# Chunk 4 of images 1 to 6: loads of u and z placed behind a transposed tile, a transpose of u moved from step 10 to step 24

## The chip, the cores and the metric

The kernel runs on one core of one Trainium2 chip. The metric is the device time of one execution in microseconds (us); lower is better. Five engines work side by side, each through its own queue in order: PE (TensorE, matrix products; its weight loads are listed as PEld), DVE (VectorE), ACT (ScalarE), POOL (GpSimd) and SP (SyncE, which only issues transfers). Transfers (DMAs) are issued from the queues of SP, POOL and ACT and land later; whoever needs the data waits for the landing.

## The reference

A gated attention unit without softmax, followed by a two-layer network with a quick GELU, over 8 images of 3008 tokens:

```python
# u, v: (8, 3008, 256), z: (8, 3008, 64), w_in: (256, 2048), w_out: (2048, 256)
scores = (1.0 / S) * np.matmul(z, z.transpose(0, 2, 1))
attn = np.maximum(scores, 0.0) ** 2
out = np.matmul(attn, v)
x = (u * out).reshape(B * S, D)

h = x @ w_in
g = h * (1.0 / (1.0 + np.exp(-1.702 * h)))
return (g @ w_out).astype(np.float32)
```

The scores are symmetric, since queries and keys are both z. The result has float32 elements, 24064 x 256.

## The kernel before, in words

The images (b = 0 to 7) go one after the other. The 3008 query rows of an image are six chunks of 512 rows (i = 0 to 5, NCH = 6), the last one padded; the keys are NJ = 24 blocks of 128. For each pair of blocks a *unit* (i, jp) of scores is made: PE multiplies (L246), ACT takes the ReLU into a tile rl (L267; L257 for a folded half), DVE squares it into a tile a (L272, L281, L284; L258 for the half). Because the scores are symmetric, half of the blocks are not computed a second time but turned by transposing DMAs on SP's queue: `turn_unit` (L309) writes the tiles tt, L274 the tile ad, L288 the tile al. For chunk 4 the turned units are jp = 10 and jp = 11; they fill the first and the second half of the tile TT[b, 4, 5].

The order of the work is written out by hand. `attend` gives the steps of a chunk (matmuls of the attention with v, L528); the loop over n walks through them, and tables keyed by (chunk i, step n) say what else is put in ahead of a step: SCHED how many units are taken (those of chunk 4 at (3, 3), (3, 10), (3, 17) and, with one of chunk 5, (3, 24), in the order of `pieces`), LOAD when a chunk's u is loaded (`load_u`, L206, four DMAs on POOL's queue), TURN when DVE turns it 32 by 32 (`turn_u`, L213, tile uq into ut). The list LAST2 holds the two last stores of the image before: a DVE transpose (yo, L858) and four or more DMAs on SP (L868) each.

In images 1 to 6 chunk 4 is done in another way (`split`, `attend_split`): a Strassen-like scheme of seven products P1 to P7 on sums of blocks. Its matmuls are L439. The sums of the scores, S1 to S4 (tile sa, L391 to L395; S3 in place, L382), are made on DVE at the places that `fills` lists; for the last third of the keys they are S1 at (4, 12), S2 at (4, 14), S4 at (4, 16) and (4, 18), S3 at (4, 20) and (4, 22), and they read TT[b, 4, 5]. The products end in L451 (ACT) and L457 (DVE) on tiles ya, which share their buffers with rl, and in the gates L459, L461, L453, which multiply with the turned u. In the same chunk 16 groups of the network's first layer run between the steps (`up_group`: PE L583, ACT gelu L596 into gf, DVE L602 into gt, then sums L718 to L722).

`load_z` prepares the next image. For each half of the blocks it loads z (`stage_z`, POOL's queue, L160 and L163), copies it beside itself on POOL (L173), and transposes it into ZT by a DMA on SP's queue (L174). ZT of the next image is read first by the scores that are taken in chunk 5 at step 2. `load_u` of chunk 5 stands at (4, 29); its turn is at (5, 8).

The places that matter here, for images 1 to 6:

- POOL's queue: u of chunk 4 at (3, 44); at (4, 2) z half 0, copy 0, z half 1, copy 1; u of chunk 5 at (4, 29). Each copy waits for its half's landing. Before it, POOL has a marker (L88) that waits for PE in the middle of chunk 3.
- SP's queue around the start of chunk 4: four stores, ad, two halves of tt, two of al, the next stores, the two transposes of ZT.
- DVE's queue: yo of the first store, then the squares of chunk 4's units; the turn of u at (4, 10), ahead of S1.

Of the kernel before, what the change touches and what calls it, by code (L numbers as in the profile page):

```python
# [10 lines left out]
F16 = mybir.dt.float16  # L11
P = 128
# [3 lines left out]
def kernel(  # L16
# [20 lines left out]
    NJ = (S + P - 1) // P  # L37
# [3 lines left out]
    NCH = (S + CH - 1) // CH  # L41
    CB = CH // P
    NU = NJ // 2
# [12 lines left out]
    dve, act, pe, sp, pool = nc.vector, nc.scalar, nc.tensor, nc.sync, nc.gpsimd  # L56
# [9 lines left out]
    pw = ctx.enter_context(tc.tile_pool(name="pw", bufs=2))  # L66
# [14 lines left out]
    ZT, V16, UQ, UT, XT, unit, TT = {}, {}, {}, {}, {}, {}, {}  # L81
# [74 lines left out]
    def stage_z(b, n0, **home):  # L156
        zst = ZS[n0] = pw.tile([P, NU, 2, DQK], F16, name="zst", **home)
        full = min(NU, NJ - 1 - n0)
        src = z[b, n0 * P:(n0 + full) * P].rearrange("(n p) d -> p n d", p=P)
        pool.dma_start(zst[:, :full, 0, :], src)  # L160
        if full < NU:
            for h in range(2):
                pool.dma_start(zst[h * SREM:(h + 1) * SREM, full, 0, :], z[b, S0:S])  # L163

    def load_z(b):
        ZT[b] = pz.tile([P, NJ, P], F16, name="ZT", tag="ZT")
        if b == 1:
            stage_z(b, NU, tag="y")
        for n0 in range(0, NJ, NU):
            if b > 1:  # L170
                stage_z(b, n0, tag="y")
            zst = ZS[n0]
            pool.tensor_copy(zst[:, :, 1, :], zst[:, :, 0, :])  # L173
            sp.dma_start_transpose(ZT[b][:, n0:n0 + NU], zst.rearrange("p n c d -> p (n c d)"))  # L174
# [24 lines left out]
    def load_u(b, i):  # L199
        eng = pool if b else sp  # L200
        n = width(i)
        uq = pu.tile([P, CH // QW, QW, NCC], F32, name="uq", tag="uq")
        src = u[b, i * CH:i * CH + n].rearrange("(q t) c -> t q c", t=QW)
        for k in range(P // QW):
            cs = slice(k * NCC * QW, (k + 1) * NCC * QW)
            eng.dma_start(uq[k * QW:(k + 1) * QW, :n // QW].rearrange("t q c k -> t q (c k)"), src[:, :, cs])  # L206
        UQ[b, i] = uq
# [22 lines left out]
    def turned(b, i):  # L230

        return i < NCH - 1 and (b > 0 or i > 3)
# [102 lines left out]
    def split(b, i):  # L335

        return i == NCH - 2 and 0 < b < B - 1
# [127 lines left out]
    def fills(b):  # L465

        VT.clear()
        SA.clear()
        at = {(0, 19): [lambda: pool.tensor_copy(VZ[TOP], V16[b][TOP, NJ - 1])]}
        slots = [(0, n) for n in (20, 23, 26, 28)] + [(1, n) for n in (27, 31, 35, 39, 43)]  # L470
        slots += [(2, n) for n in (19, 21, 23)]
        ops = [op for t in range(3) for op in value_forms(b, t)]
        slots += [(2, n) for n in (28, 33, 38, 43)] + [(3, n) for n in (30, 34, 41, 44)]
        slots += [(4, n) for n in (12, 12, 14, 14, 16, 18, 20, 22)]
        ops += [op for t in range(3) for op in score_forms(b, t)]
        assert len(ops) == len(slots)
        for where, op in zip(slots, ops):
            at.setdefault(where, []).append(op)
        return at

    def full(b):

        return NCH - 2 if b < B - 1 else NCH - 1
# [349 lines left out]
    LAST2 = []  # L833
# [42 lines left out]
    def pieces(b, i):  # L876

        lst = [(i, jp) for jp in range(2 * i, NU)]
        if i == NCH - 1:
            return [(i, jp) for jp in range(2 * i) if not turned(b, jp // 2)] + lst  # L880
        if b == 0:
            return lst[-2:] + lst[:-2] if turned(b, i) else lst
        if split(b, i):
            return [lst[0], lst[2], lst[3], lst[1]]
        k = max(len(lst) - 6, 2)
        return lst[:k] + lst[-2:] + lst[k:-2]

# [12 lines left out]
    TURN0 = {(i, (38, 28)[i] if i < 2 else NJ + 4 if i < NCH - 1 else 12): i for i in range(NCH)}  # L900
    LOAD0 = {(1, 14): 2, (1, 40): 3, (4, 4): 4, (4, 36): 5}
    TURN = {(1, NJ + 4): 2, (2, NJ + 4): 3, (4, 10): 4, (5, 8): 5}
    LOADW = {
        (2, 16): 0, (3, 0): 2, (3, 9): 1, (3, 41): 3, (4, 28): 4, (4, 34): 5, (4, 40): 6, (5, 0): 7,
    }
    CASTW = {(3, 8): 0, (3, 40): 2, (4, 8): 1, (4, 14): 3}
    LOAD = {(3, NJ + 20): 4, (4, NJ + 5): 5}

    FIRST_ZT, FIRST_CAST = {12: 4, 20: 5}, {5: 4, 13: 5}
    SCHED0 = {  # L910
# [14 lines left out]
    def fill(b):  # L925
        assert not queue
        queue.extend(u_ for i in range(NCH) for u_ in pieces(b, i))
# [28 lines left out]
    for b in range(B):  # L956
        nup = NCH * NFG
        more = b + 1 < B
        sched = SCHED0 if b == 0 else SCHED if more else SCHED_LAST
        turn, load = (TURN, LOAD) if b else (TURN0, LOAD0)  # L960
        head = 0
        for i in range(NCH):
            host = b + 1 if more and i == NCH - 1 else b
            if host > b:
                fill(host)
                LATE.append(host)
            if i == 0 and split(b, NCH - 2):
                extra = fills(b)
            for n, step in enumerate(attend_split(b, i) if split(b, i) else attend(b, i, b == 0 and i == 0)):
                if b == 0 and i == 0 and n in (5, 24):  # L970
                    load_u(0, n // 24)
                if b == 0 and i == 0 and n == 2:
                    copies = first_zt(3)
                if b == 0 and i == 0 and n == 3:
                    copies()
                if b == 0 and i == 0 and n in FIRST_CAST:
                    first_cast(FIRST_CAST[n], True)
                if b == 0 and i == 0 and n in FIRST_ZT:
                    first_zt(FIRST_ZT[n])()
                if (i, n) in turn:  # L980
                    turn_u(b, turn[i, n])
                if (i, n) in ((3, 3), (3, 26) if more else (4, 14)) and LAST2:
                    LAST2.pop(0)()
                if (i, n) == (0, 22) and COPY:
                    COPY.pop(0)()
                if (i, n) in load:
                    load_u(b, load[i, n])
                if b == 0 and (i, n) in CASTW:
                    cast_w(CASTW[i, n])
                if b == 0 and (i, n) in LOADW:  # L990
                    load_w(LOADW[i, n])
                if b == 0 and (i, n) == (NCH - 2, 6):
                    stage_z(1, 0, tag="yo", bufs=1)
                if more and (i, n) == (NCH - 2, 2 if b else 16):
                    load_z(b + 1)
                if b == 0 and i == NCH - 1 and n in (8, 30, 42):
                    wsums.pop(0)()
                take(host, sched[i].get(n, 0))
                if split(b, NCH - 2):
                    for op in extra.get((i, n), ()):  # L1000
                        op()
                if split(b, i):
                    step()
                if i == full(b) and n >= HEAD and (n - HEAD) * LAGY // (2 * NJ - 10) >= head and head < LAGY:
                    up_group(b, head)
                    head += 1
                if not split(b, i):
                    step()
        late.sort(key=lambda t: t[0])
        if more:  # L1010
            for i in range(2):
                load_u(b + 1, i)
            for n0 in range(0, NJ, VB):
                load_v(b + 1, n0)
        prods = products(b)
        for q in range(head, nup):
            if more and q in (head + 14, head + 20):
                k = int(q == head + 20)
                turn_u(b + 1, k)
                load_u(b + 1, k + 2)  # L1020
            up_group(b, q)
            if b == 0 and q == head + 3:
                wsums.pop(0)()
            prods.pop(0)()
            for a_ in AFTER:
                a_[0] -= 1
            while AFTER and AFTER[0][0] < 0:
                AFTER.pop(0)[1]()
            if q >= 44 and late:
                late.pop(0)[1]()  # L1030
        steps = prods
        for step in steps:
            step()
            for sum_ in [SUMS.pop(0) for _ in range(min(len(SUMS), 1 + (len(SUMS) > 4)))]:
                sum_[2]()
            for _, turn_it in [late.pop(0) for _ in range(min(len(late), 1 + (len(steps) < 10)))]:
                turn_it()
        LATE.clear()
        if more:
            while late:  # L1040
                late.pop(0)[1]()
            take(b + 1, 2)
# [30 lines left out]
```

## Time and profile before

Three runs took 1172.9, 1173.56 and 1173.79 us; the median is 1173.56.

| what | value |
|---|---|
| the profiled execution | 1173.48 us |
| its span, from the first instruction to the last | 1171.4 us |
| granted TensorE clock | 1.000 |
| first L439 matmul of chunk 4, images 1 to 6 | 205.16, 350.43, 493.34, 638.32, 780.48, 927.60 us |
| landing of a tt transpose after its issue, all 232 | 3.1 / 3.4 / 11.5 us (min / median / max) |
| u load, one of four: POOL's time to issue it | 649 ns (median) |
| turn of u on DVE, 48 of them | 1236 ns (median) |
| POOL's copy of a z half, 14 of them | 958 ns (median) |

Lines of the profile name a line of the kernel, an engine, an operation, the tile written and the tiles read, the count, and times. In the list of waits the columns are: who waited, for whom, us in total, how often, the longest one. In a table of windows each row is a stretch of time, followed by each engine's busy time and instructions, the granted clock, the share of the DMA engines and their rate. In a timeline each row is a start, a duration, an engine, a line, an operation and, in brackets, the engine's idle time before it and what ended it. An engine's idle time costs nothing unless PE comes to wait for it: PE is busy 99% of the span.

### The profile page before, as it was taken

The page shows a single profiled execution, that of the slowest core. Times are in us where ns is not written, and L with a number is a line of the kernel's source. Part 1 is how long each engine was busy: PE and PEld are TensorE (multiplying, and loading weights), DVE is VectorE, ACT ScalarE, POOL GpSimd, SP SyncE. Part 2 cuts the span into 40 slices and gives each one's busy share as a digit, 9 for nine tenths or more (in the row PEclk, how much of TensorE's full clock was granted, in tenths as well). Part 3 has the DMA queues.
Part 4 walks back from the last instruction along what each step waited for, and adds up shares of the span by engine and source line. Part 5 has one row for each costly group of instructions (what it writes and reads, how often), then busy time and mean ns, then how long its engine had stood idle before and what let it go on. Part 6 is the DMA issues. An engine that isn't in the chain of part 4 may idle for free.

```text
span 1171.4 us, 21514 instructions
## 1 busy us (share of the span) xinstructions
PE 1163.4 (99%) x8212; PEld 590.0 (50%) x8212; DVE 961.4 (82%) x1596; ACT 841.9 (72%) x959; POOL 215.2 (18%) x301
## 2 busy tenths in 40 slices
PE   9999999999999999999999999999999999999998
PEld 3544455644455445554445545555444554544446
DVE  7789878988789886899868997779977899664776
ACT  7888864788647886478864787657876588672785
POOL 3033201232012320142101421014210241001000
PEclk9999999999999999999999999999999999999999
DMA  9996399854998559976499655995559955697023
GB/s 222 201 168 96 79 172 158 100 94 92 169 156 101 90 108 170 153 104 87 97 172 153 107 86 111 170 139 103 90 101 170 153 106 85 119 165 142 1 36 73
DMA packets 459032, 143.53 MB, mean 123 GB/s; under 512 B 424624, under 2 KB 453040, under 8 KB 458928
## 3 DMA queue, kind: packets, MB, share of 16 engines
q1 hardware_dynamic: 402464, 102.36, 53.6%
q0 software_dynamic: 55104, 38.49, 21.8%
q8 instruction: 64, 1.05, 0.4%
q10 hardware_dynamic: 1360, 1.31, 0.4%
q14 instruction: 40, 0.33, 0.1%
HBM read 60.29 MB, written 24.64 MB: 73 GB/s over the span
## 4 chain that ended last, share of the span: by engine, by line
PE 92%; DVE 3%; DMA 3%; ACT 1%; issue 1%; SPq 0%; DVEq 0%; ACTq 0%
PE o L528 32%; PE hg L583 26%; PE st L756 23%; PE sc L246 6%; PE oz L439 4%; DMA tt<-a 2%; PE st L804 1%; PE yp L730 1%; DVE gt L602 1%; DMA out_dram<-yo 1%; ACT rl L267 1%; ACT gf L596 0%; DVE vt L362 0%; SPq L868 0%; PE w L101 0%
## 5 line engine op out<-in xcount | busy, mean ns | idle before, releaser
L596 ACT ACTIVATE gf<-hg 128x1024 f32<-128x1024 f32 (+1 forms) x384 | 383.4, 1002 | 119.7 <-PE hg L583 100.0
L267 ACT ACTIVATE rl<-sc 128x1024 f16<-128x1024 f32 (+1 forms) x301 | 288.8, 992 | 153.7 <-PE sc L246 109.9
L583 PE MATMUL hg<-xt,W 128*128 128x512 f16 (+1 forms) x1408 | 353.5, 374 | 0.2
L528 PEld LDWEIGHTS <-V 64*128 64x128 f16 (+1 forms) x3810 | 206.6, 94 | 201.1 <-POOLq L88 6.1
L528 PE MATMUL o<-a,V 64*128 64x512 f16 (+3 forms) x2254 | 290.5, 368 | 0.4 <-DVE a L281 0.4
L602 DVE TENSOR_SCALAR gt<-gf 128x1024 f16<-128x1024 f32 (+1 forms) x288 | 204.8, 712 | 66.4 <-ACT gf L596 63.7
L206 POOL DMA_DIRECT2D uq<-in_u_dram x168 | 117.2, 706 | 725.4 <-DVE a L284 394.1
L281 DVE TENSOR_TENSOR a<-rl 128x1024 f16<-128x1024 f16 (+1 forms) x266 | 176.2, 673 | 77.2 <-ACT rl L267 76.1
L583 PEld LDWEIGHTS <-W 128*128 128x128 f16 x1536 | 149.4, 98 | 156.5 <-issue 3.3
L528 PE MATMUL o<-tt,V 64*128 64x512 f16 (+1 forms) x1278 | 166.9, 376 | 0.0
L246 PE MATMUL sc<-ZT 64*128 64x512 f16 (+3 forms) x688 | 117.3, 356 | 0.7 <-ACT ZT L145 0.3
L756 PEld LDWEIGHTS <-WT 128*128 128x128 f16 x736 | 71.9, 98 | 79.6 <-issue 0.6
L600 ACT ACTIVATE gt<-gf 128x1024 f16<-128x1024 f32 (+1 forms) x96 | 98.1, 1022 | 3.1
L756 PE MATMUL st<-gt,W 128*128 128x512 f16 (+1 forms) x368 | 89.9, 370 | 0.0
L756 PE MATMUL st<-s,WT 128*128 128x512 f16 (+1 forms) x368 | 89.1, 370 | 0.0
L756 PE MATMUL st<-gt,WT 128*128 128x512 f16 (+1 forms) x368 | 88.8, 370 | 0.0
L756 PEld LDWEIGHTS <-W 128*128 128x128 f16 x552 | 53.8, 98 | 58.3
L858 DVE STREAM_TRANSPOSE yo<-y 128x1024 f32<-128x1024 f32 (+1 forms) x46 | 56.0, 1218 | 8.5 <-DMA out_dram<-yo 5.8
L718 DVE TENSOR_TENSOR s<-gt 128x1024 f16<-128x1024 f16 (+1 forms) x92 | 61.3, 666 | 1.1
L720 DVE TENSOR_TENSOR s<-s,gt 128x1024 f16<-128x1024 f16 (+1 forms) x92 | 61.0, 663 | 1.2
L773 DVE SCALAR_TENSOR_TENSOR y<-st,y 128x512 f32<-128x512 f32 (+1 forms) x69 | 45.7, 662 | 19.6 <-PE st L756 18.8
L722 DVE TENSOR_TENSOR s<-gt,s 128x1024 f16<-128x1024 f16 (+1 forms) x92 | 59.4, 657 | 2.2 <-DVE s L720 1.4
(100 smaller groups left out, 916.8 us busy)
## 6 DMA issues: line engine op xcount, KB each, us to landing
out_dram<-yo SPq DMA_DIRECT2D x156, 128.0 KB, 2.8
uq<-in_u_dram POOLq DMA_DIRECT2D x140, 128.0 KB, 3.5
V<-in_v_dram POOLq DMA_DIRECT2D x35, 256.0 KB, 6.0
tt<-a SPq DMA_TRANSPOSE x232, 3.4
uq<-in_u_dram POOLq DMA_DIRECT2D x28, 112.0 KB, 4.6
out_dram<-yo SPq DMA_DIRECT2D x28, 96.0 KB, 3.5
uq<-in_u_dram SPq DMA_DIRECT2D x20, 128.0 KB, 4.3
wst<-in_moe_w_in_dram POOLq DMA_DIRECT2D x4, 512.0 KB, 5.1
```

The costliest lines, as they stand in the source:

```text
L206: eng.dma_start(uq[k * QW:(k + 1) * QW, :n // QW].rearrange("t q c k -> t q (c k)"), src[:, :, cs])
L246: pe.matmul(sc[:, r, :q1 - q0], zt[h, 2 * kp + r, :], zt[h].rearrange("d n p -> d (n p)")[:, q0:q1], start=True, stop=True,)
L267: act.activation(rl[:, :, :n], sc[:, :, :n], AF.Relu, scale=csc)
L281: dve.tensor_tensor(a[:, :, :n], rl[:, :, :n], rl[:, :, :n], ALU.mult)
L528: ins = pe.matmul(acc[c][:, :n], channels(V16[b][h, j], c), weights(b, i, j)[h], start=(k, m) == first[c], stop=(k, m) == final[c],)
L583: pe.matmul(hg[:, e, :n], W1[:, c, ff * P:(ff + 1) * P], XT[b, i][:, c, :n], start=(c == 0), stop=(c == NCC - 1),)
L596: act.activation(gf[:, :, :n], hg[:, :, :n], AF.Gelu_apprx_sigmoid, scale=1.0 / FSC)
L600: act.activation(g, gf[:, :, :n], AF.Copy, scale=FSC)
L602: dve.tensor_scalar(g, gf[:, :, :n], FSC, None, ALU.mult)
L718: dve.tensor_tensor(s_, a21, a22, ALU.add)
L720: dve.tensor_tensor(s_, ST[b, s, "S1", m], a11, ALU.subtract)
L756: pe.matmul(bank, right[:, ff], lhs[:, f], start=new and ff == 0, stop=ff == NFF // 2 - 1, skip_group_check=True,)
```

## The change

In six places:

- `load_z` for images 2 and up: both z halves are loaded first; then come copy 0, transpose 0, copy 1, transpose 1. It is called at (4, 4) instead of (4, 2).
- The order of chunk 4's units is 8, 11, 10, 9 instead of 8, 10, 11, 9, so that the second half of TT[b, 4, 5] is turned first.
- u of chunk 4 is loaded at (4, 4) instead of (3, 44).
- Ahead of that, at (4, 4), POOL copies one element per partition of each half of TT[b, 4, 5] into a new tile hold. POOL thus waits for the landing of both halves, and the loads of u and z, which come after it in its queue, with it.
- u of chunk 4 is turned at (4, 24) instead of (4, 10).
- The first of the stores in LAST2 comes at (3, 4) instead of (3, 3), behind the unit that is taken at (3, 3).

All hold while images 1 to 6 run; the last one in image 7 too. No product is added or left out.

```diff
--- before.py
+++ after.py
@@ -166,9 +166,10 @@
         ZT[b] = pz.tile([P, NJ, P], F16, name="ZT", tag="ZT")
         if b == 1:
             stage_z(b, NU, tag="y")
+        if b > 1:
+            for n0 in range(0, NJ, NU):
+                stage_z(b, n0, tag="y")
         for n0 in range(0, NJ, NU):
-            if b > 1:
-                stage_z(b, n0, tag="y")
             zst = ZS[n0]
             pool.tensor_copy(zst[:, :, 1, :], zst[:, :, 0, :])
             sp.dma_start_transpose(ZT[b][:, n0:n0 + NU], zst.rearrange("p n c d -> p (n c d)"))
@@ -881,7 +882,7 @@
         if split(b, i):
-            return [lst[0], lst[2], lst[3], lst[1]]
+            return [lst[0], lst[3], lst[2], lst[1]]
@@ -900,11 +901,13 @@
     TURN = {(1, NJ + 4): 2, (2, NJ + 4): 3, (4, 10): 4, (5, 8): 5}
+    TURNS = {(1, NJ + 4): 2, (2, NJ + 4): 3, (4, 24): 4, (5, 8): 5}
...
     LOAD = {(3, NJ + 20): 4, (4, NJ + 5): 5}
+    LOADS = {(4, 4): 4, (4, NJ + 5): 5}
@@ -958,6 +961,8 @@
         turn, load = (TURN, LOAD) if b else (TURN0, LOAD0)
+        if split(b, NCH - 2):
+            turn, load = TURNS, LOADS
@@ -979,10 +984,13 @@
                 if (i, n) in turn:
                     turn_u(b, turn[i, n])
-                if (i, n) in ((3, 3), (3, 26) if more else (4, 14)) and LAST2:
+                if (i, n) in ((3, 4), (3, 26) if more else (4, 14)) and LAST2:
                     LAST2.pop(0)()
...
+                if split(b, i) and n == 4:
+                    hold = pw.tile([P, 2], F16, name="hold", tag="hold")
+                    pool.tensor_copy(hold, TT[b, i, NCH - 1][:, ::2, 0, 0])
                 if (i, n) in load:
                     load_u(b, load[i, n])
@@ -991,7 +999,7 @@
-                if more and (i, n) == (NCH - 2, 2 if b else 16):
+                if more and (i, n) == (NCH - 2, 4 if b else 16):
                     load_z(b + 1)
```

## The prediction

> **What bounds the kernel now.** I read the page first. TensorE (PE) is busy throughout; the engines that feed it have slack on average.
>
> ```profile
> PE 1163.4 (99%) x8212; PEld 590.0 (50%) x8212; DVE 961.4 (82%) x1596; ACT 841.9 (72%) x959; POOL 215.2 (18%) x301
> PE 92%; DVE 3%; DMA 3%; ACT 1%; issue 1%; SPq 0%; DVEq 0%; ACTq 0%
> ```
>
> The second line, the chain that ended last, is PE's too. The change removes no matmul, so it can only win PE's stalls in the places that it touches: chunk 4 of images 1 to 6. To price these I laid one window on each image, from the first matmul of L439 (the start of chunk 4; "+x" below is us after it) to +32.42, in chunk 5.
>
> ```profile
> core 0: us, PE busy (x) PEld busy (x) DVE busy (x) ACT busy (x) POOL busy (x), PEclk, DMA share, GB/s
> 205.16:237.58 32.42, 32.42 (x246) 19.78 (x246) 29.55 (x52) 23.63 (x27) 9.66 (x14) 1.00 0.81 102
> 350.43:382.85 32.42, 32.28 (x241) 19.36 (x241) 29.73 (x51) 23.21 (x26) 9.24 (x14) 1.00 0.87 104
> 493.34:525.76 32.42, 32.42 (x248) 19.18 (x248) 29.89 (x53) 24.07 (x27) 10.74 (x15) 1.00 0.91 104
> 638.32:670.74 32.42, 32.42 (x248) 19.16 (x248) 30.97 (x55) 23.82 (x27) 11.14 (x15) 1.00 0.79 112
> 780.48:812.90 32.42, 31.14 (x226) 18.22 (x226) 29.12 (x51) 21.98 (x25) 8.28 (x11) 1.00 0.90 96
> 927.60:960.02 32.42, 32.42 (x248) 19.18 (x248) 30.31 (x54) 24.06 (x27) 11.22 (x15) 1.00 0.72 107
> ```
>
> The clock is 1.00 everywhere. Images 3, 4 and 6 place 248 matmuls, images 1, 2 and 5 place 246, 241 and 226: these three are late. How late follows from the window starts. From an odd image to the next: 145.27 (image 1), 144.98 (3), 147.12 (5); from an even one: 142.91 (2), 142.16 (4). Images 3 and 4 being clean, image 1 lost 0.29, image 2 0.75, image 5 2.14 us: **3.18 us in all, the most that the change can win.**
>
> Then the waits of image 5, and the landing of the transposed tile tt, for the two tt transposes just before chunk 3's end (193 to 199 us, no load beside them) and for those of image 5's chunk 4.
>
> ```profile
> POOL zst L173 <- DMA zst<-in_z_dram: 17.1, 2, 11.2
> ...
> ACT gf L596 <- DVE gt L602: 3.9, 2, 2.9
> PEld L439 <- issue: 2.4, 4, 1.4
> DVE sa L391 <- DMA tt<-a: 1.7, 1, 1.7
> ...
> PE oz L439 <- DVE sa L391: 1.2, 1, 1.2
> ```
> ```profile
> DMA to landing us min/median/max: 4.1/4.4/4.7
> ```
> ```profile
> DMA to landing us min/median/max: 10.0/10.8/11.5
> ```
>
> VectorE (DVE) waits 1.7 us for the tile, PE then 1.2 us for the sum made of it. The same DVE wait is 0.62 us in image 1 and 0.58 in image 2, none in 3, 4 and 6. The two halves of tt are issued near -3.0 and -1.6, and the four u loads (POOL, -4.5 to -1.9) and the first z half (-1.9) lie beside them.
>
> **The change, part by part.**
>
> *Loads behind the landing.* The copy into hold reads both halves of tt, so POOL waits until both have landed. Its own price is bounded by the 186 ns of the 128x1 copy at L635; nothing else of POOL's is queued there but u, z and, later, chunk 5's u. Bounds for the landing of tt: 4.1 us from issue (the clean pair), or 11.5 (nothing improves). I take 4.4, nearer in kind: the same two transposes without loads.
>
> [...]
>
> *First store a step later, halves of tt swapped.* On DVE the 1.24 us yo transpose now runs after unit 8's square (0.65), and SP issues the ad transpose (1.4) ahead of the four stores (2.1) instead of behind. The tt transposes stay behind both, so they move ahead by at most about 1 us (SP's former wait). The second yo transposes when the first stores have landed; in images 4 and 6 it already sat idle 2.17 and 1.75 us before it and both images are clean, so up to that a delay is covered by PE's queue of ready tiles. Swapping puts first the half that S1 reads. Cost nothing, gain nothing beyond the wait; without the cover, as in image 5, it would cost PE up to 1.2 us an image.
>
> *What is late next: z and the second u.* With tt issued near -3 and landing by +1.5: four u issues at 0.65 bring POOL to +4.1, then z's issues 1.06 + 1.06 + 2 x 0.57 to +7.4. Landing of a z DMA was 3.1 to 10.5 us; the last halves of images 2, 4 and 6 took some 4 to 5, those of 1, 3 and 5 some 6 to 7, with a ZT transpose beside them. I take 4.7: +12.1, then the second copy (0.9) to +13.0. Formerly it ran at +11.5 (image 6) to +19.2 (image 5). ZT is first read at +23.5, chunk 5's u turned at +27.4: covered by 5 us and more.
>
> *The turn of u, from step 10 to step 24.* One STREAM_TRANSPOSE, 1.24 us, 1.16 from its start to the next one's. Moved, not added; but the places differ. Around step 10 DVE idles before each gt (0.55 to 0.82 us), so the turn was nearly free. Step 24 lies ahead of the gt at 942.99 in image 6's timeline:
>
> ```profile
> 941.45 0.69 DVE L602 TENSOR_SCALAR gt<-gf 128x1024 f16<-128x1024 f32 x1
> 942.06 0.68 DVE L718 TENSOR_TENSOR s<-gt 128x1024 f16<-128x1024 f16 x1
> 942.66 0.41 DVE L382 TENSOR_TENSOR ad<-ad 128x512 f16<-128x512 f16 x1
> 942.99 0.68 DVE L602 TENSOR_SCALAR gt<-gf 128x1024 f16<-128x1024 f32 x1
> ...
> 945.78 0.69 DVE L602 TENSOR_SCALAR gt<-gf 128x1024 f16<-128x1024 f32 x1 [0.23 <-ACT gf L596]
> 946.39 0.42 DVE L457 TENSOR_TENSOR ya<-ya,oz 128x256 f32<-128x256 f32 x1
> 947.08 0.69 DVE L602 TENSOR_SCALAR gt<-gf 128x1024 f16<-128x1024 f32 x1 [0.28 <-ACT gf L596]
> ```
>
> The gt at 941.45 (+13.85) starts on ACT's word, so what the turn saved earlier is lost there. After it starts stand 0.60 apart (0.33 after a half-size one); only 0.06 + 0.30 + 0.36 = 0.72 us of idle follows, and none from 947.08 to the square L272 at 954.09 (+26.5). Inserting 1.16 makes L272 late by 1.16 - 0.72 = 0.44.
>
> What a late L272 costs PE, the late images tell: the ReLU that waits for L272 starts at +27.26 in image 6, +27.78 in image 1, +28.28 in image 2, +29.59 in image 5; late by 0.52, 1.02, 2.33, where PE lost 0.29, 0.75, 2.14. **The first 0.25 us are free, the rest goes to PE one to one**, as the score banks come free late. So 0.44 - 0.25 = 0.19 in five images. In image 2 the trace has that ReLU wait for the instruction after L272, L258 (0.33 us on): 0.44 + 0.33 - 0.25 = 0.52 there. Together 5 x 0.19 + 0.52 = 1.5 us. Bounds: 0 (0.72 a little larger) and 0.91 an image (no idle used, 1.16 - 0.25).
>
> **Sum.** 1173.48 (this execution; its span is 1171.4, 2.1 lie around it) - 3.18 + 1.5 = 1171.8; image 2's longer wait is one observation and may be gone in another order of waits (1171.5), and I take 1171.6. The median of the runs, 1173.56, stands 0.08 above, which I leave. That is -0.17%, beside the 0.2% (2.35 us) that a measurement of this kernel tells from no change.
>
> **Rivals.**
>
> *The turn costs nothing (0.12):* ACT's gelu waits shrink too and give DVE 0.2 us more idle. For it: image 1 lost little with 0.52 of lateness. Against: DVE has no idle from 947.08 on. 1173.48 - 3.18 = 1170.3.
>
> *z falls on the busy DVE (0.25), the one on the other side.* Place: the stretch from +13.85 to +26.5. A POOL copy of z beside a two-input DVE instruction took L718 from 0.68 to 1.31 us in image 1 (221.64): +0.62; the u issues that follow it made two gt of image 2 0.80 and 0.87 instead of 0.68: +0.30. If the second copy lands there in every image, lateness is 0.44 + 0.62 + 0.30 = 1.36, PE loses 1.11 x 6 = 6.7, time 1177.0; with the copy alone 0.81 x 6 = 4.9, time 1175.2. It breaks even at a lateness of 0.25 + 3.18 / 6 = 0.78 and is slower by 0.2% from 0.25 + 5.53 / 6 = 1.17. For it: the hold puts z's first issue from -1.9 to about +4, and a z landing of 6 us instead of 4.7 is enough. Against: the second half no longer waits for the first one's landing and copy (its issue stood at +5.9 to +11.1, now +5 to +7).
>
> *The hold doesn't quicken tt (0.08):* stores and the other transposes, not the loads, are what delays it. For: the stores share SP's queue with it. Against: the pair with 4.4 us has transposes beside it as well. Then the wait stays and the loads come later: 1173.5 to 1174.5.
>
> **How the numbers follow.** Forecast 0.55, own range 1170.4 to 1172.6; 0.29 of it lies below 1171.2, 0.26 above. Faster: 0.29 + 0.12 = 0.41. Same: 0.26 + 0.08 + 0.08 (z late in the copy alone) = 0.42. Slower: 0.17 (z late with its company). Range: from 1170.0, under which no stall is left to win, to 1174.8, which leaves out most of the z case.
>
> **What would show it.** Right: the waits "DVE sa <- DMA tt" gone in all six images, tt landing within 5 us of its issue, six equal window counts a little under 248, a new DVE stretch without idle from +13.85, L272 near +26.9. The turn is mis-sized if L272 stands at +26.5 or after +27.3. The z case shows as DVE instructions of 1.3 us after +13.85. Wrong altogether if PE stalls where these windows don't look: the end of chunk 3, or the scores at +23.5 waiting for ZT.

## The result, and the profile after

The changed kernel took a median of 1175.95 us (1175.28 to 1178.72, nine runs), the kernel before 1173.51 us (1170.48 to 1174.4, nine runs): a ratio of 1.0027 with a 95% interval of 1.0017 to 1.0038. That is slower by 0.27%, past the 0.2% named (the interval reaches down to 0.17%; the two medians alone give 1.0021), and above the predicted range. The profiled execution took 1175.55 us with a span of 1173.7, at a granted clock of 1.00. The lines named here have moved by one, from L173 on: L174 is POOL's copy of z, L440 is the matmul of chunk 4, L458 the sum ya, L603 the gt, L273 the first square of chunk 5's scores, L214 the turn of u.

The page's busy times and its chain of waits, after:

```profile
PE 1165.0 (99%) x8212; PEld 593.6 (51%) x8212; DVE 961.8 (82%) x1596; ACT 842.4 (72%) x959; POOL 220.3 (19%) x307
PE 90%; DVE 6%; ACT 2%; issue 1%; DMA 1%; SPq 0%; DVEq 0%; ACTq 0%
```

DMA has gone from 3% of the chain to 1%, as meant; DVE has gone from 3% to 6%. The same six windows of 32.42 us from the start of chunk 4, after:

```profile
core 0: us, PE busy (x) PEld busy (x) DVE busy (x) ACT busy (x) POOL busy (x), PEclk, DMA share, GB/s
205.15:237.57 32.42, 32.18 (x242) 19.60 (x242) 30.60 (x53) 23.35 (x26) 14.61 (x20) 1.00 0.83 100
350.79:383.21 32.42, 32.18 (x241) 19.38 (x241) 30.63 (x53) 23.23 (x26) 13.66 (x20) 1.00 0.71 106
493.72:526.14 32.42, 32.26 (x244) 19.65 (x244) 30.76 (x54) 23.53 (x27) 13.81 (x20) 1.00 0.78 102
639.14:671.56 32.42, 32.18 (x242) 19.59 (x242) 30.88 (x53) 23.34 (x26) 14.77 (x20) 1.00 0.73 104
781.97:814.39 32.42, 31.44 (x232) 19.00 (x232) 30.84 (x53) 22.50 (x25) 14.23 (x18) 1.00 0.69 102
928.51:960.93 32.42, 32.07 (x240) 19.41 (x240) 31.26 (x53) 23.06 (x26) 14.55 (x19) 1.00 0.77 105
```

No image places 248 matmuls any more; images 3, 4 and 6, which were clean, now place 244, 242 and 240. What each image lost follows as in the prediction, from one window's start to the next less the undisturbed 144.98 (odd images) or 142.16 (even ones), and for image 6 from its start to the start of PE's last matmul less 239.55, which is what the trace of before has there. Images 1 to 6 lost 0.67, 0.76, 0.45, 0.67, 1.56 and 0.93 us, together 5.04, where before they lost 0.28, 0.75, 0, 0, 2.14 and 0, together 3.18. The difference is 1.86. Another 0.45 lies at the very end of the program: from the start of the last matmul to the end of the span 4.69 us pass instead of 4.24, because POOL's closing DRAIN ends later (it starts 0.30 us later and takes 0.25 us instead of 0.11). What makes it do so is open. The two together are the 2.3 by which the spans differ.

The part of the change that was meant to win did so. The landing of the two tt transposes of image 5's chunk 4, after:

```profile
DMA to landing us min/median/max: 3.8/3.9/4.0
```

It was 10.0 to 11.5. The list of waits no longer has DVE waiting for tt. It has these instead (who waited for whom, us in total, times, the longest):

```profile
ACT gf L597 <- DVE gt L603: 24.0, 31, 1.7
POOL zst L174 <- DMA zst<-in_z_dram: 23.3, 12, 4.6
DVE yo L859 <- DMA out_dram<-yo: 15.0, 6, 3.3
...
PE oz L440 <- DVE ya L458: 1.0, 6, 0.2
PE hg L584 <- ACT gf L597: 0.8, 2, 0.6
```

The fourth line is new: in all six images PE waits for the sum ya of product P7 (1.0 us in all), because in the kernel the first matmul of P4 writes the tile oz that this sum reads. Image 4's timeline, DVE and POOL from +10.5 on (its chunk 4 starts at 639.14):

```profile
649.65 0.41 DVE L396 TENSOR_TENSOR sa<-tt,sa 128x512 f16<-128x512 f16 x1
650.38 0.69 DVE L603 TENSOR_SCALAR gt<-gf 128x1024 f16<-128x1024 f32 x1 [0.32 <-ACT gf L597]
650.99 1.05 DVE L396 TENSOR_TENSOR sa<-tt,sa 128x512 f16<-128x512 f16 x1
651.96 0.68 DVE L603 TENSOR_SCALAR gt<-gf 128x1024 f16<-128x1024 f32 x1
652.57 1.04 DVE L383 TENSOR_TENSOR a<-a 128x512 f16<-128x512 f16 x1
653.52 0.68 DVE L603 TENSOR_SCALAR gt<-gf 128x1024 f16<-128x1024 f32 x1
654.13 0.68 DVE L719 TENSOR_TENSOR s<-gt 128x1024 f16<-128x1024 f16 x1
654.73 0.41 DVE L383 TENSOR_TENSOR ad<-ad 128x512 f16<-128x512 f16 x1
655.07 1.23 DVE L214 STREAM_TRANSPOSE ut<-uq 128x1024 f32<-128x1024 f32 x1
```
```profile
650.59 1.17 POOL L174 COPY zst<-zst 128x768 f16<-128x768 f16 x1 [2.75 <-DMA zst<-in_z_dram]
652.04 1.28 POOL L174 COPY zst<-zst 128x768 f16<-128x768 f16 x1 [0.28 <-DMA zst<-in_z_dram]
```

The last sum of S4 takes 1.05 us and the first of S3 1.04, while the same operations take 0.41 at 649.65 and 654.73; the two slow ones lie under the two copies of z. The gt that the forecast expected at +13.85 on ACT's word starts at +14.38 (653.52) with no idle time before it, and the turn at +15.93. L273 follows at +27.39.

A copy beside such a sum is not new, and by itself it need not cost time. In the kernel before, image 4's second copy stood at the same place (its chunk 4 starts at 638.32) and stretched the same sum of S3, at +13.43, to 1.04 us; yet image 4 was clean. The turn stood at step 10 there.

```profile
651.75 1.04 DVE L382 TENSOR_TENSOR a<-a 128x512 f16<-128x512 f16 x1
```
```profile
651.14 1.37 POOL L173 COPY zst<-zst 128x768 f16<-128x768 f16 x1 [3.08 <-DMA zst<-in_z_dram]
```

In image 4 of the changed kernel, the P4 matmul, with its wait, at 659.66:

```profile
659.20 0.41 DVE L458 TENSOR_TENSOR ya<-ya,oz 128x256 f32<-128x256 f32 x1
...
659.66 0.38 PE L440 MATMUL oz<-tt,vt 128*128 128x256 f16 x2 [0.17 <-DVE ya L458]
```

In image 5 there is a second thing, early in the chunk:

```profile
782.32 0.98 DVE L859 STREAM_TRANSPOSE yo<-y 128x768 f32<-128x768 f32 x1 [3.28 <-DMA out_dram<-yo]
```
```profile
787.96 1.94 ACT L597 ACTIVATE gf<-hg 128x1024 f32<-128x1024 f32 x2 [1.72 <-DVE gt L603]
```

DVE sat 3.28 us before the second yo transpose, which waits for the landing of the first stores. The gates and the first gt come late by it, ACT waits 1.72 us for gt, and PE, at hg, for ACT: from one matmul to the next 0.87 us pass at 788.16.

### The profile page after: what moved, and what is told of

Same layout as the page of the kernel before. It is cut to its first block, busy times and chain, and to the rows that moved or that the text cites. A ratio compares the mean times of both kernels' runs of the same rounds, so it can differ in the third digit from the quotient of the medians.

```text
span 1173.7 us, 21529 instructions
## 1 busy us (share of the span) xinstructions
PE 1165.0 (99%) x8212; PEld 593.6 (51%) x8212; DVE 961.8 (82%) x1596; ACT 842.4 (72%) x959; POOL 220.3 (19%) x307
## 3 DMA queue, kind: packets, MB, share of 16 engines
q8 instruction: 64, 1.05, 0.4%
## 4 chain that ended last, share of the span: by engine, by line
PE 90%; DVE 6%; ACT 2%; issue 1%; DMA 1%; SPq 0%; DVEq 0%; ACTq 0%
PE o L529 33%; PE hg L584 24%; PE st L757 23%; PE sc L247 6%; PE oz L440 2%; DVE gt L603 2%; PE st L805 1%; ACT gf L597 1%; DVE s L719 1%; PE yp L731 1%; DVE ut L214 1%; DMA tt<-a 1%; ACT rl L268 0%; DVE s L721 0%; DVE sa L396 0%
## 5 line engine op out<-in xcount | busy, mean ns | idle before, releaser
L603 DVE TENSOR_SCALAR gt<-gf 128x1024 f16<-128x1024 f32 (+1 forms) x288 | 204.8, 713 | 65.2 <-ACT gf L597 63.5
L247 PEld LDWEIGHTS <-ZT 64*128 64x128 f16 x688 | 39.8, 94 | 44.6 <-issue 9.3
```

The costliest lines, as they stand in the source:

```text
L247: pe.matmul(sc[:, r, :q1 - q0], zt[h, 2 * kp + r, :], zt[h].rearrange("d n p -> d (n p)")[:, q0:q1], start=True, stop=True,)
L603: dve.tensor_scalar(g, gf[:, :, :n], FSC, None, ALU.mult)
```

## Experiments

Three suspects remain: **T**, the turn of u at step 24; **C**, POOL's copies of z, both of which now lie between +11.0 and +15.4, beside DVE's sums; **S**, the first store a step later. They were taken away one by one and together. Each "lost" below is read from that run's own trace as above, in us; "end" is what the end of the program takes beyond the 4.24 us of before.

| kernel | turn | copies of z | first store | lost, images 1 to 6 | sum | end | median us | ratio to before, 95% |
|---|---|---|---|---|---|---|---|---|
| before | 10 | POOL | 3 | 0.28 0.75 0 0 2.14 0 | 3.18 | 0 | 1173.51 | |
| changed | 24 | POOL | 4 | 0.67 0.76 0.45 0.67 1.56 0.93 | 5.04 | 0.45 | 1175.95 | 1.0027 (1.0017 to 1.0038) |
| e1 | 16 | POOL | 4 | 0.38 0.70 0 0.53 1.02 0.52 | 3.15 | 0.43 | 1173.38 | 1.0006 (0.9991 to 1.002) |
| e3 | 24 | POOL | 3 | 0.70 0.67 0.77 0.91 0.63 0.80 | 4.48 | 0.43 | 1175.28 | 1.0019 (1.0006 to 1.0032) |
| e4 | 16 | POOL | 3 | 1.62 0.01 0.07 0.39 0.26 0.46 | 2.81 | 0.44 | 1173.02 | 0.9995 (0.9981 to 1.0009) |
| e5 | 24 | none | 4 | 0.22 0.55 0.22 0.30 1.49 0.21 | 2.99 | 0.02 | 1172.76 | 0.9994 (0.9985 to 1.0003) |
| e6 | 16 | none | 3 | 0.39 0 0 0.01 0 0 | 0.40 | 0.01 | 1170.59 | 0.9972 (0.9961 to 0.9984) |
| e2: before, turn late | 24 | POOL | 3 | 0.51 0.97 0.97 1.11 2.69 0.41 | 6.65 | 0 | 1176.47 | 1.0032 (1.0018 to 1.0047) |
| e7: z alone moved | 10 | POOL | 3 | 0 0.32 0.01 0 0.29 0.17 | 0.79 | 0.44 | 1171.98 | 0.9986 (0.9974 to 0.9999) |
| e8: as e7 | 10 | POOL | 3 | 0 0.26 0.06 0 0.67 0 | 1.00 | 0.45 | 1172.18 | 0.9991 (0.9982 to 1.0001) |

The spans less these sums and ends lie between 1167.8 and 1168.7 in all ten kernels, so the six stretches and the end hold nearly all the differences. Between single profiles up to 1 us comes from elsewhere (e6 reaches image 1's chunk 4 at 205.69 us, e5 at 204.74). Each row's losses are those of one profiled execution. In e7 and e8 that execution took about 1 us less than the median, so theirs are the losses of a good run; in the others it lies within 0.6 us of the median. Each ratio is to runs of before taken in the same round: their median was 1173.0 for e1 to e4 and 1173.36 for e5 to e8.

**e1_turn16.** The changed kernel with the turn of u at step 16.

```diff
-    TURNS = {(1, NJ + 4): 2, (2, NJ + 4): 3, (4, 24): 4, (5, 8): 5}
+    TURNS = {(1, NJ + 4): 2, (2, NJ + 4): 3, (4, 16): 4, (5, 8): 5}
```

> The changed kernel with one edit: u of chunk 4 is turned at step 16 instead of 24, where DVE still waits for the gelus. Theory T (the late turn): in the changed kernel the turn at step 24 makes DVE's sum of P7 late, and PE waits for it at the first matmul of P4 (list of waits: 1.0 us, 6 times; against an undisturbed image each such place costs PE 0.33 us) and, in images 1, 4, 5, 6, for a gelu that waits for gt (0.2 to 0.4 us each). T expects both to vanish: some 3.3 us less than the changed kernel, 1172.0 to 1172.6, ratio to before about 0.999. Rival C (the z copies): POOL's two copies, now at +11 to +14.6, slow S4, S3 and a gt by 0.6 us each and are the cause; they stay, so the wait for the P7 sum stays in most images and the time is 1174.5 to 1176. Rival S (the store a step later) expects 1175 to 1176 too, with the loss in images 5 and 6 near +6.

Measured: 1173.38 us, 2.57 below the changed kernel's median, between what T and what C expected. The wait of PE for ya is gone from the list of waits; smaller delays remain at that matmul, 0.20 to 0.29 us in images 1, 2, 5 and 6, where each image of the changed kernel had 0.32 or 0.33. Four images still lose 0.5 to 1.0 us. So the turn's place is a part of the cost, and something that does not depend on it is another.

**e2_before_turn24.** The kernel before, in which only the turn goes from step 10 to step 24, in images 1 to 6.

```diff
         turn, load = (TURN, LOAD) if b else (TURN0, LOAD0)
+        if split(b, NCH - 2):
+            turn = {(1, NJ + 4): 2, (2, NJ + 4): 3, (4, 24): 4, (5, 8): 5}
```

> The kernel before with one edit: in images 1 to 6 u of chunk 4 is turned at step 24 instead of 10; loads, stores and order as before. Theory T: the wait of PE for the P7 sum appears in all six images, 6 x 0.33 = 2.0 us, some gelu waits with it, while the waits for tt mostly stay (S1 comes 1.2 us earlier on DVE, so they grow rather than shrink): 1175 to 1177, ratio 1.0015 to 1.003. Rival C: a lateness of 0.44 us alone lies within PE's cover; PE does not wait for the sum, 1173.5 to 1174.5.

Measured: 1176.47 us, and the two waits side by side in its list of waits:

```profile
PE oz L439 <- DVE ya L457: 2.4, 5, 1.0
DVE sa L391 <- DMA tt<-a: 1.7, 2, 1.5
```

The late turn alone makes the kernel before slower by about as much as the whole change does (the intervals of the two ratios overlap), and it brings PE's wait for ya with it, as T expected. The images that were clean, 3, 4 and 6, now lose 0.97, 1.11 and 0.41. In those of e2, too, POOL's copies lie beside DVE's work: the second one stretches a gt to 1.32 us (image 3, +17.7) and a sum to 1.04 (image 4, +15.2), so this run does not price the turn by itself.

**e3_store33 and e4_turn16_store33.** The changed kernel with the first store back at step 3; e4 has the turn at step 16 as well.

```diff
-                if (i, n) in ((3, 4), (3, 26) if more else (4, 14)) and LAST2:
+                if (i, n) in ((3, 3), (3, 26) if more else (4, 14)) and LAST2:
```

> The changed kernel with one edit: the first store of LAST2 back at step 3 of chunk 3. Rival S: the second yo transpose of DVE (which waited 3.3 us for the stores in image 5) comes earlier, the waits of PE for a gelu near +6 in images 5 and 6 (0.65 and 0.38 us) go: 1174.5 to 1175.0. Theory T: the P7 waits stay at 1.0 us in the list, so no more than that is won; ratio to before still 1.001 to 1.002.

> The changed kernel with both edits: turn at step 16, first store at step 3 of chunk 3. T and S together expect the undisturbed pace in all six images: 1170.3 to 1171.3, ratio 0.997 to 0.9985. Rival C expects the P7 waits to stay: 1173.5 to 1175.

Measured: 1175.28 and 1173.02 us. In e3 PE's gaps near +6 are gone and image 5 loses 0.63 instead of 1.56; images 3 and 4 lose 0.2 to 0.3 more than in the changed kernel, so one image's number is good to about that. The gaps went as S expected; the time stayed just above its range. In e4 images 2 and 3 are clean and images 4 to 6 are not. Its 1.62 in image 1 has a cause of its own: u landed only at +11.9 there, the turn at step 16 waited for it until +12.0, and DVE's queue with it. T and S together are thus not the whole cost, and the time lies between what T and S together and what C expected.

**e5_z_by_dma.** The changed kernel, in which z is loaded twice, into both columns of the staging tile, and POOL copies nothing (image 1's z, which comes earlier, keeps its copy).

```diff
+        for c in range(1 + both):
-        pool.dma_start(zst[:, :full, 0, :], src)
+            pool.dma_start(zst[:, :full, c, :], src)
...
-                stage_z(b, n0, tag="y")
+                stage_z(b, n0, both=True, tag="y")
...
-            pool.tensor_copy(zst[:, :, 1, :], zst[:, :, 0, :])
+            if b == 1:
+                pool.tensor_copy(zst[:, :, 1, :], zst[:, :, 0, :])
```

> The changed kernel, with the second half of each z staging tile filled by a second DMA from z instead of POOL's copy (turn of u at step 24 as changed). Theory C (POOL's two z copies beside DVE's two-input sums are what makes the squares late): the sums S4 and S3 near +12 and +13.4 take 0.41 us instead of 1.04, the gt of unit 8 is back at +13.85, L273 stands near +26.9, PE's gaps before P4 shrink from 0.43 to under 0.2 us, and the time falls by 1.5 to 2.5 us, to 1173.0 to 1174.0. Theory T (the place of the turn alone does it): the gaps of 0.43 us before P4 stay in all six images and the time stays within 0.5 us of 1175.5.

Measured: 1172.76 us, 3.2 below the changed kernel and a little under C's range. Image 4's timeline on DVE (chunk 4 starts at 637.85; L398, L385, L605 and L216 are the changed kernel's L396, L383, L603 and L214):

```profile
649.70 0.42 DVE L398 TENSOR_TENSOR sa<-tt,sa 128x512 f16<-128x512 f16 x1
650.39 0.69 DVE L605 TENSOR_SCALAR gt<-gf 128x1024 f16<-128x1024 f32 x1 [0.27 <-ACT gf L599]
651.00 0.42 DVE L385 TENSOR_TENSOR a<-a 128x512 f16<-128x512 f16 x1
651.69 0.87 DVE L605 TENSOR_SCALAR gt<-gf 128x1024 f16<-128x1024 f32 x1 [0.27 <-ACT gf L599]
...
653.41 1.23 DVE L216 STREAM_TRANSPOSE ut<-uq 128x1024 f32<-128x1024 f32 x1
```

The two sums are back at 0.42 us, the gt at 651.69 is at +13.84 and starts on ACT's word again, the turn stands at +15.56. In images 1 and 3 L273 starts at +26.95, where the forecast had +26.9. One part of the expectation did not come true: in image 4 PE's gap before P4 is still 0.31 us from matmul to matmul, and in images 1, 2, 3 and 5 it is 0.24 or 0.25, not under 0.2. Images 2 and 5, and these two alone by more than 0.1, lose more than the others' 0.22: they have PE gaps of 0.43 us (image 2, at hg, +6.2) and of 0.58 and 0.91 (image 5, +4.7 and at hg, +6.7), and in the list DVE's yo still waits 15.5 us.

**e6_turn16_store33_z_by_dma.** All three taken out: e5 with the turn at step 16 and the first store at step 3.

> The changed kernel with all three suspects taken out: turn of u at step 16, first store back at step 3, z's second half by DMA. If T, C and S are all of the cost, each of the six images runs at the undisturbed pace but for the turn of image 1, and the time is 1170.3 to 1171.3. If C costs nothing, it is the time of the same kernel with the copies, 1173.0. If POOL's longer row of DMA issues (3.3 us more) delays z and chunk 5's u, ZT lands after +23.5 and the scores wait: above 1173.5.

Measured: 1170.59 us (1169.62 to 1171.03), faster than both kernels. Its windows:

```profile
205.69:238.11 32.42, 32.19 (x244) 18.95 (x244) 28.40 (x52) 23.58 (x27) 16.39 (x21) 1.00 0.88 117
351.05:383.47 32.42, 32.42 (x248) 19.20 (x248) 29.94 (x53) 24.06 (x27) 17.73 (x22) 1.00 0.91 120
493.21:525.63 32.42, 32.42 (x248) 19.18 (x248) 29.42 (x52) 24.05 (x27) 18.12 (x22) 1.00 0.85 117
638.19:670.61 32.42, 32.42 (x248) 19.18 (x248) 30.42 (x54) 23.94 (x27) 17.30 (x22) 1.00 0.94 122
780.36:812.78 32.42, 32.42 (x248) 19.18 (x248) 29.50 (x53) 24.05 (x27) 17.55 (x22) 1.00 0.85 120
925.35:957.77 32.42, 32.42 (x249) 19.19 (x248) 30.19 (x55) 24.06 (x27) 17.73 (x22) 1.00 0.99 122
```

Five images place their 248 matmuls. Image 1 loses 0.39: u landed at +11.4 and the turn started at +11.5. POOL's longer row of issues (17 us busy instead of 14 in the window) costs nothing: L273 is at +26.48 to +26.50 in images 2 to 6, as in the clean images of before (+26.48 to +26.55).

**e7_z_alone and e8_u_early.** Of the change, only z goes behind the landing of tt (hold at step 4, both halves loaded first, the two units swapped); u is loaded before the chunk and turned at step 10, and the first store is at step 3, as before. e8 puts the load of u 14 steps earlier.

```diff
-    TURNS = {(1, NJ + 4): 2, (2, NJ + 4): 3, (4, 24): 4, (5, 8): 5}
+    TURNS = {(1, NJ + 4): 2, (2, NJ + 4): 3, (4, 10): 4, (5, 8): 5}
-    LOADS = {(4, 4): 4, (4, NJ + 5): 5}
+    LOADS = {(3, NJ + 20): 4, (4, NJ + 5): 5}
```

(in e8 the last line has `(3, NJ + 6)`)

> Only z goes behind the landing of tt (hold at step 4, both halves staged, halves of tt swapped); u is loaded before the chunk's end and turned at step 10 as before the change, first store at step 3. If the u loads by themselves delay tt, tt lands 8 to 11 us after its issue, DVE waits for it in images 1, 2 and 5 as before and the time is 1173.0 to 1174.0. If z's loads were the delay, tt lands within 5 us, the turn is free at step 10, and the time is 1170.3 to 1171.5.

> As the run with z alone behind the landing, but u is loaded 14 steps earlier in chunk 3, so that it has landed before tt is issued, and is turned at step 10. If loads beside tt are what delays it and the late turn is what cost the change its gain, tt lands within 5 us, DVE waits for nothing before +12, PE stalls only by the z copies (0.2 to 0.4 us an image at most), and the time is 1170.3 to 1172.0, the best of all. Rival: the early u lies beside chunk 3's own transposes and makes them late, and PE stalls in chunk 3: 1173.5 or more.

Measured: 1171.98 and 1172.18 us. In e8 every engine executes the same instructions in the same order as in e7, and u was still issued at -4.48: its place in the program did not move its issue. So e8 is a second look at e7 and says nothing on an early u. As to e7, neither expectation was met whole. The landing of tt in its image 5:

```profile
DMA to landing us min/median/max: 9.0/9.4/9.7
```

Over the six images it took 5.5 to 9.7 us, slower than the changed kernel's 3.1 to 4.2 with no load beside it; the kernel before has 6.4 to 11.5 over its six images, beside u and z. No wait of DVE for tt is left in the list of waits. Whether z or the swap of the halves took it away is not separated. S1 reads the second half of TT[b, 4, 5] and, without the wait, would have stood ready at about +8.0, +8.2 and +8.8 in images 1, 2 and 5 of the kernel before. In e7 the later of the two halves landed at +7.70 at the latest. But in the kernel before the half issued first landed at +6.28, +6.07 and +7.36 in these images: had that been the half that S1 reads, it would have been in time too. No run swaps the halves alone. With the turn at step 10 two copies of z still slow two DVE instructions in each image (for example two sums of 1.04 us in image 1, which loses nothing), and three images lose 0.17 to 0.32.

No run shows the late turn with neither of the other two, the late store with neither, z alone moved without POOL's copies, the halves swapped alone, or the kernel before without POOL's copies.

## Why the prediction was wrong

By its own steps:

- **What there was to win** was right. The waits for tt are in none of the six images any more, and e6 wins 2.8 of the 3.18 us (3.18 less 0.40).
- **The landing of tt, the hold, the times of z** were right. The halves of tt landed at +0.2 to +2.7 (forecast: by +1.5), z's last load at +12.8 to +14.5 (forecast +12.1). Two figures beside them were off, without weight in the sum: the copy into hold took 0.39 us on average, where 0.19 was named as its bound, and the landings of z, given as 3.1 to 10.5 us, reach 12.2 over the whole execution of before. The rival "the hold doesn't quicken tt" fell: tt landed 3.1 to 4.2 us after its issue in all six images, where before it took 6.4 to 11.5.
- **The turn's cost** was right in size. Without the copies (e5), images 1, 3 and 6 lose 0.21 or 0.22 each where 0.19 was worked out, with L273 at +26.95 and +26.93; image 2's 0.55 looked like the 0.52, but it has a gap at hg near +6, which the forecast did not mean. Laid beside the clean images of before, matmul by matmul, e5's six images lose 1.3 us at P4 and at the scores behind it, forecast 1.5.
- **"The first 0.25 us are free, the rest goes to PE one to one"** held as a rule of size. In the changed kernel L273 stood at +27.39, +27.22, +27.16, +27.39, +28.28, +27.65; less 26.48 and less 0.25 this is 0.66, 0.49, 0.43, 0.66, 1.55, 0.92, against 0.67, 0.76, 0.45, 0.67, 1.56, 0.93 lost: five images within 0.02, image 2 by 0.27 above it. The stall's place was mostly wrong: PE loses nearly all of this before L273, at P4's first matmul and at hg, most of it some 7 to 9 us before. Waits of the scores are 0.09 us in each image, near +25, and in image 2 alone another 0.25 at +29.4, where the matmul waits for ACT's ReLU: that is the place that the forecast meant.
- **The step that failed most: "the second copy (0.9) to +13.0 ... covered by 5 us and more".** The copies were priced by who reads them, ZT, and not by whom they slow. They ran between +11.0 and +15.4 and took two DVE instructions per image from 0.41 to 1.04 us or from 0.69 to as much as 1.35. Beside the late turn and the late store that is 5.04 - 2.99 = 2.05 us of stalls, set at nothing; the 0.43 at the program's end went with the copies too. The rival "z falls on the busy DVE" had the mechanism. That it had nearly the time as well (1175.2) was partly luck, as it priced neither the store nor the end, and it had a wrong place: it looked only at the stretch from +13.85 on, whereas the stretch before it, with DVE's idle of about 0.3 us ahead of each gt, was taken as harmless. With the turn at step 10 it could be: image 4 of before is clean. With the late turn it isn't: the slowed sums use that idle up and start the late stretch late (by 0.5 us in image 4), on top of the turn.
- **The second term set at nothing: "Cost nothing, gain nothing beyond the wait"**, for the first store a step later. The cover named there, yo's idle time, was not enough in image 5: "up to 1.2 us" was the price without it, and e5's image 5 lost 1.27 more than the 0.22 of the turn, image 2 0.33 more. The size of the cover was about right: in the changed kernel the images in which yo waited 2.2 to 2.4 us lost next to nothing near +6, while image 6, with 2.52, lost 0.27 and image 5, with 3.28, 0.77. What was wrong is that the delay would stay within it. With the store back (e3) the gaps near +6 are gone. About 1.7 us in e5 and 1.1 in the changed kernel; the share of S without the other two was not run.

Summed anew: 1173.48 - 3.18 + 1.3 (turn) + 1.7 (store) + 2.05 (copies) + 0.45 (end) = 1175.8, and the profiled execution took 1175.55. This is no check on the terms: the first two are e5's 2.99 divided by place, and the third is the rest up to the changed kernel's 5.04. Nor are they independent. Taken back one at a time from the changed kernel, the turn's place (e1) wins 1.89 us of stalls, the copies (e5) 2.05, the store (e3) 0.56. The turn wins more there than the 1.3 that it costs without the copies, probably since both draw on the same idle of DVE.

## What to carry to other kernels

A moved transfer brings its followers along: price a copy behind it not only by who waits for its result, but by which engine is slowed while it runs (here DVE, whose 128x512 sums went from 0.41 to 1.04 us beside POOL's copies), and look for that engine's work at the new time. Idle time ahead of an instruction that starts on another engine's word (here 0.2 to 0.4 us of DVE's ahead of a gt) can be spent once; add up everything that is moved into the stretch before calling any one of them covered. And where a change bundles moves, the part that wins can be had alone: here the loads behind the landing, with the halves swapped, z's second half by DMA and the turn and the store kept early (e6), beat both kernels.

## What the runs showed of the hardware

- A transposing DMA (tt) of images 1 to 6's chunk 4 landed 3.1 to 4.2 us after its issue with no load beside it (changed kernel), 5.5 to 9.7 beside the four u loads (e7), and 6.4 to 11.5 beside u and z (before; 10.0 and 11.5 in image 5).
- In the changed kernel each of the seven 128x512 sums of DVE that took 1.04 or 1.05 us instead of 0.41 lay under a POOL copy of z, and a copy took up to 1.35 us instead of 0.82 (spans on POOL are rough); in e5 and e6, where these copies are gone, no sum between +11 and +15 took more than 0.42. The gt was stretched as well, from 0.69 to as much as 1.35 us under a copy. A gt beside POOL's issues of DMAs was longer than 0.69 us too: 0.90 to 0.94 us near +7 to +8 in the changed kernel, beside those of z, and 0.81 to 1.20 us for the slowest gt of each chunk 4 in e6, where these copies are gone.
